# Attention backward on one core: O and wo transposed by DMA, half of K on TensorE

## The chip, the cores and the metric

The kernel runs on one core of a Trainium2 chip. The core has five engines that run at the same time and wait for each other through semaphores: TensorE (PE, matrix multiplies; its weight loads are shown apart as PEld), VectorE (DVE), ScalarE (ACT), GpSimd (POOL) and SyncE (SP), which here issues every DMA. Sixteen DMA engines move data between HBM and the on-chip memory SBUF, and from SBUF to SBUF; a DMA can transpose 128x128 blocks of two-byte data on its way through the crossbar. Matmuls write PSUM, eight banks, from which DVE or ACT copies results to SBUF.

The metric is the device time in microseconds. Of the kernel before there are three runs, median 1665.89 us.

## The reference

Two independent attention blocks A and B, forward and gradients. Only one block's forward is shown; the reference runs it for A and B, concatenates both outputs on the last axis, and takes the gradients of all ten inputs for a given `grad_out`.

```python
B, Sq, D = 8, 96, 640
H, Sk, Dh = 32, 512, 128
q = transpose((x @ wq).reshape(B, Sq, H, Dh), (0, 2, 1, 3))
scores = einsum("bhqd,bhkd->bhqk", q, k_cache) * Dh ** -0.5
p = softmax(scores)
o = einsum("bhqk,bhkd->bhqd", p, v_cache)
out = transpose(o, (0, 2, 1, 3)).reshape(B, Sq, H * Dh) @ wo
...
_out, _vjp = jax.vjp(forward, A_x, A_k_cache, A_v_cache, A_wq, A_wo, B_x, B_k_cache, B_v_cache, B_wq, B_wo)
return (_out, *_vjp(grad_out))
```

All data are bfloat16. The gradients are those of x, of both caches, of wq and of wo.

## The kernel before

One unit of work is a head h and a batch b: 96 queries against 512 keys, 512 units in all (2 blocks x 32 heads x 8 batches). The code does not write instructions in their final order at once. It puts closures into a list, each with a tick and a slot (`Emitter`, L16), sorts by tick and slot and runs them (L25). Unit number n of a block has the tick `ct = tick0 + 8 h + b`, so each head is eight ticks long, and the stages of one unit are spread over the ticks that follow by the table `OFF` (L45): scores at ct+3 (`c_s2a`, `c_s2b`), normalised probabilities at ct+3 (`c_s3b`, on POOL), the transposed probabilities and dV at ct+4 (`c_s45`, `c_s4`), the output O at ct+5, dP and dS at ct+6 (`c_s6`), dK and the transpose of dS at ct+7 (`c_s7`, `c_s8`), dQ at ct+8. In one tick TensorE so works on six units at different stages. A scheduler keeps this order on each engine but for the scores' stages, which have a higher priority, and DMAs marked `pinned` keep the order in which they stand.

Per head there is more work, spread by the table `HK` (L46), whose numbers are ticks relative to the head's first: loads of the head's slices of wq and wo (`pA` at -10, `pA2` at -9), their transposes (`pB` at -3), the projections Q and dO (`pC`), their transposes (`pD`), the transposes of O and dQ to rows of tokens (`qA`, at 18 and 17), and with these the gradients of wo (`qB` at 19 and 20) and of wq (`qD`, for two heads together). Ticks of 8 and more fall into the next heads. For every group of four or five heads there are the matmuls that add the heads' parts to `out` and `dx` (`gU`, L503), spread over some 18 ticks after the group's last unit; stretches of ticks with and without these alternate.

K and V are loaded for two batches at a time: K five ticks ahead of its unit (`OFF["ldk"]`), V three. Both are needed transposed as well. V is always transposed by a DMA from SBUF to SBUF (`c_xt`, tile VT, at the tick of the unit, read six ticks later at L417). For K there are two ways, and `k_on_pe` (L556) chooses: a DMA too (tile KT, three ticks ahead of the unit, read at L298), or TensorE with an identity matrix (`c_s1`, L285, into PSUM, then a DVE copy to the tile KT_pe, L287). Before the change, TensorE has batches 0 and 1 of every head and all batches of the first heads (A0, A1 and B0), which makes 146 of 512; the DMA has 183 pairs of batches.

wo of a head is a tile wo_h of 128x640, that is five blocks. `pB` transposes it on TensorE (L210), and ACT copies the result from PSUM to woT_h (L212, one buffer), which `pC` reads as weights for dO (L243). O of a head is 128x768 in one of the slots of the tile OD, that is six blocks; `qA(h, 0)` transposes it on TensorE (L455), ACT copies it to Onat (L456, one buffer), and `qB` reads it one and two ticks later for dwo (L469).

Order and queues: all DMAs stand in SP's one queue, in the order of their ticks and slots, loads and transposes in slots 0 to 1.7 of a tick. Before it issues a DMA, SP waits for the semaphores of what it needs: the data (an ACT or DVE copy, or an earlier DMA), the buffer's last reader (mostly PE), and the eighth DMA before, since eight semaphores are used in turn. What stands behind a waiting DMA waits with it. PSUM tiles come from one pool of eight banks (`bank`, L98).

Of the kernel before, what the change touches and what calls it, by code (L numbers as in the profile page):

```python
# [11 lines left out]
BF16 = mybir.dt.bfloat16  # L12
# [28 lines left out]
SL_HEAD = 90  # L41
# [1 line left out]
SL_SETUP = 96  # L43

OFF = dict(ldk=-5, ldv=-3, kt=-3, vt=0, s2=3, s3=3, s4=4, s5=5, s6=6, s7=7, s8=8)  # L45
HK = dict(pA=-10, pA2=-9, pB=-3, pC0=[-2, 0], pC1=[-1, 0], pD1=1, pD0=2, qA0=18, qA1=17, qB=[19, 20], qD=[(18, 0, 2), (19, 2, 4), (21, 4, 5)])  # L46
EV = dict(pB0="act", pB1="dve", pC00="act", pC01="act", pC10="act", pC11="dve", pD0="dve", pD1="dve", qA0="act", qA1="dve", qB0="act", qB1="dve", qD="dve", gU="act")
GSPREAD0 = 9
PRIO_OFF = 2000
# [4 lines left out]
def build_block(tc, em, tick0, blk, x, kc, vc, wq, wo, g_all, out_all, dx, dk, dv, dwq, dwo, ident, ones, pools, HG=6, first=True, groups=None):  # L54
    nc = tc.nc
# [42 lines left out]
    def bank(shape, dt, name):  # L98
        return ps.tile(shape, dt, name=name, tag="bank")
# [55 lines left out]
    def evac(eng, dst, src, sc=None):  # L155
        if eng == "act":
            nc.scalar.activation(dst, src, ACT.Identity, scale=(1.0 if sc is None else sc))
        else:
            if sc is None:
                nc.vector.tensor_copy(dst, src)  # L160
            else:
                nc.vector.tensor_scalar(dst, src, float(sc), None, op0=ALU.mult)
# [33 lines left out]
    def pA2(h):  # L196
# [5 lines left out]
            HS[(blk, h)]["wo_h"] = wo_h  # L202
        return f

    def pB(h):
        def f():
            st = HS[(blk, h)]
            woT_ps = bank([128, DC * 128], BF16, "woT_ps")
            for c in range(DC):
                nc.tensor.transpose(woT_ps[:, c * 128:(c + 1) * 128], st["wo_h"][:, c * 128:(c + 1) * 128], ident[:])  # L210
            woT_h = hd.tile([128, DC * 128], BF16, name="woT_h", bufs=1)
            evac(EV["pB0"], woT_h[:], woT_ps[:])  # L212
            st["woT_h"] = woT_h
            wqT_ps = bank([128, DC * 128], BF16, "wqT_ps")
            for c in range(DC):
                nc.tensor.transpose(wqT_ps[:, c * 128:(c + 1) * 128], st["wq_h"][:, c, :], ident[:])
            wqT_h = hst.tile([128, D], BF16, name="wqT_h")
            evac(EV["pB1"], wqT_h[:], wqT_ps[:])
            st["wqT_h"] = wqT_h
            st["slot"] = (blk * H + h) % OD.shape[2]  # L220
            st["OT_h"] = OD[:, 0, st["slot"]]
            st["dQT_h"] = OD[:, 1, st["slot"]]
            st["QT_h"] = hd.tile([128, T], BF16, name="QT_h")
            st["dOT_h"] = hd.tile([128, T], BF16, name="dOT_h")
        return f
# [199 lines left out]
    def c_s7(h, b):  # L425
# [9 lines left out]
            nc.scalar.activation(SB[(blk, h, b // 2, "k")][:, b % 2], dK_ps[:], ACT.Identity, scale=1.0)  # L435
        return f

    def qA(h, which):
        def f():
            st = HS[(blk, h)]  # L440
            src = st["OT_h"] if which == 0 else st["dQT_h"]
            if which == 0:
                dst = hd.tile([128, TT, 128], BF16, name="Onat", bufs=1)
                st["Onat"] = dst
            else:
                if h % 2 == 0:
                    st["dQnat"] = hd.tile([128, TT, 2, 128], BF16, name="dQnat", bufs=1)
                else:
                    st["dQnat"] = HS[(blk, h - 1)]["dQnat"]
                dst = st["dQnat"][:, :, h % 2, :]  # L450
            for t0 in range(0, TT, 8):
                nt = min(8, TT - t0)
                n_ps = bank([128, 8 * 128], BF16, "nat_ps")
                for i in range(nt):
                    nc.tensor.transpose(n_ps[:, i * 128:(i + 1) * 128], src[:, (t0 + i) * 128:(t0 + i + 1) * 128], ident[:])  # L455
                evac(EV["qA%d" % which], dst[:, t0:t0 + nt, :], n_ps[:, 0:nt * 128].rearrange("p (t d) -> p t d", d=128))  # L456
        return f
# [96 lines left out]
    NTS = len(tsplits)  # L554

    def k_on_pe(h, b):  # L556
        return b // NB == 0 or h == 0 or (first and h == 1)

    SX = pools["SX"]
    for g in range(NG):  # L560
        h0 = GH0[g]
        for hh in range(groups[g]):
            h = h0 + hh
            c0t = tick0 + h * B
            if not (first and h == 0):
                em.add(c0t + HK["pA"], SLOTS["LOAD"] + 1.7, pA(h))
                em.add(c0t + HK["pA2"], SLOTS["LOAD"] + 1.7, pA2(h))
            em.add(c0t + HK["pB"], SL_HEAD, pB(h))
            fh = first and h == 0
            p0, p1, d1, d0, late = HK["pC0"], HK["pC1"], HK["pD1"], HK["pD0"], 0  # L570
            if fh:
                p1, d1, d0, late = [3, 3], 3, 4, 7
            elif h == 0:
                p0, p1, d1, d0, late = [-2, 2], [0, 3], 3, 4, 7
            for si in range(NTS):
                em.add(c0t + p0[min(si, 1)], SL_HEAD, pC(h, 0, si))
                em.add(c0t + p1[min(si, 1)], SL_HEAD + late, pC(h, 1, si))
            em.add(c0t + d1, SL_HEAD + (8 if late else 0), pD(h, 1))
            em.add(c0t + d0, SL_HEAD, pD(h, 0))
            for b in range(B):  # L580
                ct = c0t + b
                if b % NB == 0:
                    em.add(tick0 - 12 if first and h == 0 and b == 0 else ct + OFF["ldk"], SLOTS["LOAD"], c_ld(h, b, "K", 7))
                    em.add(ct + OFF["ldv"], SLOTS["LOAD"], c_ld(h, b, "V", 5))
                    if not k_on_pe(h, b):
                        em.add(ct + OFF["kt"], SLOTS["LOAD"] + 1, c_xt(h, b, "KT", 3))
                    em.add(ct + OFF["vt"], SLOTS["LOAD"] + 1, c_xt(h, b, "VT", 4))
                if k_on_pe(h, b):
                    em.add(ct + 2, SLOTS["S1"], c_s1(h, b))
                em.add(ct + OFF["s2"], SLOTS["S2A"], c_s2a(h, b))  # L590
                em.add(ct + OFF["s2"], SLOTS["S2B"], c_s2b(h, b))
                em.add(ct + OFF["s3"], SLOTS["S3A"], c_s3a(h, b))
                em.add(ct + OFF["s3"], SLOTS["S3B"], c_s3b(h, b))
                em.add(ct + OFF["s5"], SLOTS["S5B"], c_s5b(h, b))
                if b % 2 == 1:
                    em.add(ct + OFF["s4"] + 1, SLOTS["LOAD"] + 1.5, c_st(h, b, "v"))
                    em.add(ct + OFF["s7"] + 1, SLOTS["LOAD"] + 1.5, c_st(h, b, "k"))
                em.add(ct + OFF["s4"], SLOTS["S4"], c_s4(h, b))
                for i, o in enumerate(("s8", "s7", "s5", "s4")):
                    SX.setdefault(ct + OFF[o], [None] * 4)[i] = (blk, h, b)  # L600
                em.add(ct + OFF["s6"], SLOTS["S6"], c_s6(h, b))
                em.add(ct + OFF["s7"], SLOTS["S7"], c_s7(h, b))
            hk = HK if first or h < H - 1 else dict(HK, qA0=13, qB=[14, 15], qA1=16, qD=[(19, 0, 2), (19, 2, 4), (19, 4, 5)])
            em.add(c0t + hk["qA0"], SL_HEAD, qA(h, 0))
            for di in range(len(wsplits)):
                em.add(c0t + hk["qB"][di], SL_HEAD + 1, qB(h, di))
            em.add(c0t + hk["qB"][-1] + 1, SLOTS["LOAD"] + 1.6, qB_st(h))
            em.add(c0t + hk["qA1"], SL_HEAD, qA(h, 1))
            for (k_, c_lo, c_hi) in hk["qD"]:
                if c_lo < DC and h % 2 == 1:  # L610
                    em.add(c0t + k_, SL_HEAD + 2, qD(h, c_lo, min(c_hi, DC)))
            if h % 2 == 1:
                em.add(c0t + hk["qD"][-1][0] + 1, SLOTS["LOAD"] + 1.6, qD_st(h))
        cLg = tick0 + (h0 + groups[g] - 1) * B + B - 1
        gs0 = max(3, (GSPREAD0 * groups[g]) // HG)
        gs1 = max(3, (GSPREAD1 * groups[g]) // HG)
        if not first and g == NG - 2:
            gs0, gs1 = 9, 9
        if g == 0:
            em.add(cLg + OFF["s5"] - 2, SL_LOAD, setup_acc)  # L620
        subs = [(0, t, gi) for t in range(TT) for gi in range(len(gsplits))] + [(1, t, gi) for t in range(TT) for gi in range(len(gsplits))]
        n_out = TT * len(gsplits)
        for i, (which, t, gi) in enumerate(subs):
            if which == 0:
                tk = cLg + OFF["s5"] + 2 + (i * gs0) // n_out
            else:
                tk = cLg + OFF["s8"] + 2 + gs0 - 3 + ((i - n_out) * gs1) // n_out
            em.add(tk, SL_GRP, gU(g, which, t, gi))
            if g == NG - 1 and gi == len(gsplits) - 1:
                em.add(tk + 1, SLOTS["LOAD"] + 1.6, gU_st(which, t))  # L630
# [124 lines left out]
```

## Time and profile before

| | |
|---|---|
| median of three runs | 1665.89 us (1665.25 to 1666.51) |
| the profiled execution's own time | 1665.33 us |
| its span, first to last instruction | 1663.6 us |
| instructions | 56195 |
| PE busy | 1645.5 us, 99% |
| ACT busy | 1393.7 us, 84% |
| DVE busy | 1301.9 us, 78% |
| POOL busy | 528.7 us, 32% |
| DMA, mean rate | 264 GB/s, 439.02 MB |
| granted TensorE clock | 1.0 throughout |

The span is the time from the first to the last instruction of one profiled execution; the rest of its time lies around it. A busy engine is one that has an instruction under way. Matmuls are pipelined: the time of one (219 ns for 128 columns in the profile) is longer than the distance to the next, so prices on TensorE are taken from start to start. The chain of waits goes back from the last instruction, at each step to what released it, or to the instruction before it on its engine; the engine with the largest share there sets the time. For a DMA the profile gives the issue on SP and the time from issue to landing. In the timeline a row is: start in us, length in us, engine, source line, operation, output<-inputs, shape, and how many of them were merged.

### The profile page before, as it was taken

Reading aid. Unit: us, or ns where it says so; the run is one execution under the profiler, and the core shown is the slowest. Engines: PE = TensorE matmul, PEld = TensorE weight load, DVE = VectorE, ACT = ScalarE, POOL = GpSimd, SP = SyncE. Lnnn points to the kernel's source line nnn. Section 1 sums busy time; section 2 is a strip of 40 time slices with the busy share of each in tenths; the row PEclk is TensorE's granted clock in tenths of the full one; section 3 lists DMA queues with packets and bytes.
Section 4 is the critical chain, followed back from the end, with each engine's and each line's share of the span. In section 5 each row is a group of like instructions: output and inputs, shape, how many; then the busy total and the mean of one; then the engine's idle time right before and its main releaser. Section 6 shows DMA issues by size and latency. Waiting matters only on the chain.

```text
span 1663.6 us, 56195 instructions
## 1 busy us (share of the span) xinstructions
PE 1645.5 (99%) x21536; PEld 1316.4 (79%) x21536; DVE 1301.9 (78%) x2978; ACT 1393.7 (84%) x3518; POOL 528.7 (32%) x1034
## 2 busy tenths in 40 slices
PE   8999999999999999999999999999999999999999
PEld 6887787787788787877878877877877877877886
DVE  6886677778787788888878867878778778787887
ACT  7999897797798797988868998977977977977975
POOL 2333233333233232333323323323322322332332
PEclk9999999999999999999999999999999999999999
DMA  9999999999999999999999999999999999999994
GB/s 269 257 283 284 255 268 280 249 277 285 217 277 279 245 272 253 276 267 251 292 263 278 294 281 272 278 273 238 276 277 229 287 253 250 258 282 252 281 264 136
DMA packets 811215, 439.02 MB, mean 264 GB/s; under 512 B 483777, under 2 KB 810945, under 8 KB 810945
## 3 DMA queue, kind: packets, MB, share of 16 engines
q1 hardware_dynamic: 810944, 435.43, 107.8%
q8 instruction: 169, 2.77, 0.7%
q14 instruction: 102, 0.83, 0.2%
HBM read 161.09 MB, written 159.12 MB: 192 GB/s over the span
## 4 chain that ended last, share of the span: by engine, by line
PE 78%; ACT 13%; issue 4%; DVE 3%; DMA 1%; POOL 0%; SPq 0%; ACTq 0%; DVEq 0%; POOLq 0%
PE o_ps L514 12%; PE q_ps L243 11%; PE dwq_ps L490 6%; PE dK_ps L432 5%; PE dV_ps L389 5%; PE dP_ps L417 5%; PE S_ps L298 5%; PE dwo_ps L469 5%; PE dst_ps L346 4%; PE x_ps L365 4%; PE x_ps L359 4%; PE x_ps L340 4%; ACT dK_sb L435 3%; ACT E_sb L310 3%; PE n_ps L258 3%
## 5 line engine op out<-in xcount | busy, mean ns | idle before, releaser
L329 POOL TENSOR_SCALAR P_sb<-E_sb,rinv 96x512 bf16<-96x512 bf16 x512 | 354.3, 692 | 1107.8 <-DVE rinv L320 1073.6
L310 ACT ACTIVATE E_sb<-S_ps,negm 96x512 bf16<-96x512 f32 x512 | 354.5, 692 | 160.4 <-DVE negm L300 156.6
L421 DVE SCALAR_TENSOR_TENSOR dS_sb<-dP_ps,dl_ps,P_sb 96x512 bf16<-96x512 f32 x512 | 380.9, 744 | 44.8 <-PE dl_ps L419 40.5
L300 DVE TENSOR_REDUCE negm<-S_ps 96x1 f32<-96x512 f32 x512 | 347.6, 679 | 45.5 <-PE S_ps L298 43.3
L435 ACT ACTIVATE dK_sb<-dK_ps 128x512 bf16<-128x512 f32 x512 | 305.8, 597 | 72.9 <-PE dK_ps L432 71.9
L392 ACT ACTIVATE dV_sb<-dV_ps 128x512 bf16<-128x512 f32 x512 | 314.8, 615 | 0.0
L378 ACT ACTIVATE PT_sb<-x_ps 128x384 bf16<-128x384 bf16 x512 | 256.5, 501 | 0.0
L514 PEld LDWEIGHTS <-OD 128*128 128x128 bf16 x1536 | 135.7, 98 | 103.3 <-issue 1.3
L389 PE MATMUL dV_ps<-dOnat_h,P_sb 96*128 96x128 bf16 x2048 | 198.0, 219 | 1.3 <-DVE dOnat_h L160 0.6
L432 PE MATMUL dK_ps<-Qnat_h,dS_sb 96*128 96x128 bf16 x2048 | 197.8, 219 | 0.0
L417 PE MATMUL dP_ps<-VT,dOT_h 128*96 128x512 bf16 x512 | 195.2, 381 | 0.0
L407 POOL TENSOR_TENSOR prod<-OD,dOT_h 128x96 bf16<-128x96 bf16 x512 | 186.4, 364 | 9.2 <-ACT OD L375 8.2
L348 DVE COPY dST_sb<-dst_ps 128x384 bf16<-128x384 bf16 x512 | 177.2, 346 | 11.9 <-PE dst_ps L346 11.6
L320 DVE RECIPROCAL rinv<-rowsum 96x1 f32<-96x1 f32 x512 | 79.9, 156 | 132.8 <-ACT E_sb L310 128.0
L346 PE MATMUL dst_ps<-ident,dS_sb 96*128 96x96 bf16 x2048 | 171.8, 206 | 2.6 <-DVE dS_sb L421 0.2
L375 ACT ACTIVATE OD<-x_ps 128x192 bf16<-128x192 f32 (+1 forms) x515 | 171.5, 333 | 3.4 <-PE x_ps L340 3.4
L359 PE MATMUL x_ps<-PT_sb,V_sb 128*128 128x96 bf16 x2048 | 172.2, 206 | 0.5 <-ACT PT_sb L378 0.5
L365 PE MATMUL x_ps<-ident,P_sb 96*128 96x96 bf16 x2048 | 171.7, 205 | 0.6 <-POOL P_sb L329 0.3
L340 PE MATMUL x_ps<-dST_sb,K_sb 128*128 128x96 bf16 x2048 | 170.7, 206 | 0.0
L340 PEld LDWEIGHTS <-K_sb 128*128 128x128 bf16 x2048 | 132.6, 98 | 32.1
L514 PE MATMUL o_ps<-wo_h,OD 128*128 128x128 bf16 (+1 forms) x768 | 141.0, 299 | 0.0
L514 PE MATMUL o_ps<-wqT_h,OD 128*128 128x128 bf16 (+1 forms) x768 | 140.0, 299 | 0.2
(75 smaller groups left out, 3224.4 us busy)
## 6 DMA issues: line engine op xcount, KB each, us to landing
out_dram<-dV_sb SPq DMA_DIRECT2D x256, 256.0 KB, 3.6
out_dram<-dK_sb SPq DMA_DIRECT2D x256, 256.0 KB, 3.8
K_sb<-in_A_k_cache_dram SPq DMA_DIRECT2D x128, 256.0 KB, 4.0
V_sb<-in_A_v_cache_dram SPq DMA_DIRECT2D x128, 256.0 KB, 3.9
K_sb<-in_B_k_cache_dram SPq DMA_DIRECT2D x128, 256.0 KB, 4.1
V_sb<-in_B_v_cache_dram SPq DMA_DIRECT2D x128, 256.0 KB, 4.0
out_dram<-dwo_sb SPq DMA_DIRECT2D x64, 160.0 KB, 3.8
out_dram<-dwq_sb SPq DMA_DIRECT2D x32, 320.0 KB, 4.2
```

The lines of the kernel that those rows point to most:

```text
L300: nc.vector.tensor_reduce(negm[:], S_ps[:], axis=AX.X, op=ALU.max, negate=True)
L310: nc.scalar.activation(E_sb[:], st["S_ps"][:], ACT.Exp, bias=st["negm"][:], scale=1.0, accum_out=rowsum[:])
L329: pinned(nc.gpsimd.tensor_scalar(P_sb[:], st["E_sb"][:], st["rinv"][:], 0.0, op0=ALU.mult, op1=ALU.add))
L340: nc.tensor.matmul(dQT_ps, st["K_sb"][:, c, :], st["dST_sb"][:, c * Sq:(c + 1) * Sq], start=(c == 0), stop=(c == KC - 1))
L378: nc.scalar.activation(PT_sb[:], PT_ps, ACT.Identity, scale=1.0)
L389: nc.tensor.matmul(dV_ps[:, c * 128:(c + 1) * 128], P_sb[:, c * 128:(c + 1) * 128], hs["dOnat_h"][:, b * 128:(b + 1) * 128], start=True, s ...
L392: nc.scalar.activation(SB[(blk, h, b // 2, "v")][:, b % 2], dV_ps[:], ACT.Identity, scale=1.0)
L417: nc.tensor.matmul(dP_ps[:], hs["dOT_h"][:, tok], st["VT"], start=True, stop=True)
L421: nc.vector.scalar_tensor_tensor(dS_sb[:], dP_ps[:], dl_ps[:, 0:1], st["P_sb"][:], op0=ALU.subtract, op1=ALU.mult)
L432: nc.tensor.matmul(dK_ps[:, c * 128:(c + 1) * 128], dS_sb[:, c * 128:(c + 1) * 128], hs["Qnat_h"][:, b * 128:(b + 1) * 128], start=True, s ...
L435: nc.scalar.activation(SB[(blk, h, b // 2, "k")][:, b % 2], dK_ps[:], ACT.Identity, scale=1.0)
L514: nc.tensor.matmul(o_ps[:], src[:, t * 128:(t + 1) * 128], rhs, start=(hh == 0), stop=(hh == groups[g] - 1))
```

## The change

Three things are changed. O of every head is transposed by a DMA from its slot in OD to Onat, issued at tick 14 of the head (13 for B's last) in slot 1.2, instead of six TensorE transposes and an ACT copy at tick 18. wo is transposed by a DMA from wo_h to woT_h, issued at tick -6, also in slot 1.2, for all heads but A's first two, which stay on TensorE; woT_h now has two buffers, and its first reader stands at tick -1. And `k_on_pe` now gives TensorE batches 4 and 5 of every head besides batches 0 and 1, so that 122 more units take that way and 61 pairs fewer go through the DMA. For B's last head the two halves of dwo move from ticks 14 and 15 to 16 and 17.

```diff
-HK = dict(pA=-10, pA2=-9, pB=-3, ..., qA0=18, qA1=17, qB=[19, 20], ...)
+HK = dict(pBT=-6, pA=-10, pA2=-9, pB=-3, ..., qT=14, qA1=17, qB=[19, 20], ...)
...
+    def woT_on_pe(h):
+        return first and h < 2
+
+    def pB_xt(h):
+        def f():
+            woT_h = hd.tile([128, DC * 128], BF16, name="woT_h", bufs=2)
+            pinned(nc.sync.dma_start_transpose(woT_h[:].rearrange("p (c k) -> p c k", k=128), HS[(blk, h)]["wo_h"][:]))
+            HS[(blk, h)]["woT_h"] = woT_h
+        return f
+
     def pB(h):
         def f():
             st = HS[(blk, h)]
-            woT_ps = bank([128, DC * 128], BF16, "woT_ps")
-            for c in range(DC):
-                nc.tensor.transpose(woT_ps[:, c * 128:(c + 1) * 128], st["wo_h"][:, c * 128:(c + 1) * 128], ident[:])
-            woT_h = hd.tile([128, DC * 128], BF16, name="woT_h", bufs=1)
-            evac(EV["pB0"], woT_h[:], woT_ps[:])
-            st["woT_h"] = woT_h
+            if woT_on_pe(h):
+                woT_ps = bank([128, DC * 128], BF16, "woT_ps")
+                for c in range(DC):
+                    nc.tensor.transpose(woT_ps[:, c * 128:(c + 1) * 128], st["wo_h"][:, c * 128:(c + 1) * 128], ident[:])
+                woT_h = hd.tile([128, DC * 128], BF16, name="woT_h", bufs=2)
+                evac(EV["pB0"], woT_h[:], woT_ps[:])
+                st["woT_h"] = woT_h
...
+    def qA_xt(h):
+        def f():
+            Onat = hd.tile([128, TT, 128], BF16, name="Onat", bufs=1)
+            pinned(nc.sync.dma_start_transpose(Onat[:], HS[(blk, h)]["OT_h"]))
+            HS[(blk, h)]["Onat"] = Onat
+        return f
+
...
     def k_on_pe(h, b):
-        return b // NB == 0 or h == 0 or (first and h == 1)
+        return b // NB in (0, 2) or h == 0 or (first and h == 1)
...
+            if not woT_on_pe(h):
+                em.add(c0t + HK["pBT"], SLOTS["LOAD"] + 1.2, pB_xt(h))
             em.add(c0t + HK["pB"], SL_HEAD, pB(h))
...
-            hk = HK if first or h < H - 1 else dict(HK, qA0=13, qB=[14, 15], qA1=16, ...)
-            em.add(c0t + hk["qA0"], SL_HEAD, qA(h, 0))
+            hk = HK if first or h < H - 1 else dict(HK, qT=13, qB=[16, 17], qA1=16, ...)
+            em.add(c0t + hk["qT"], SLOTS["LOAD"] + 1.2, qA_xt(h))
```

`qA` keeps only its part for dQ. Instruction counts follow from this: 206 transposes fewer on TensorE, 126 copies fewer on ACT, 122 copies more on DVE, 65 DMAs more in SP's queue.

More of the change, by code (lines that the diff above doesn't have):

```diff
@@ L45 @@
 OFF = dict(ldk=-5, ldv=-3, kt=-3, vt=0, s2=3, s3=3, s4=4, s5=5, s6=6, s7=7, s8=8)
-HK = dict(pA=-10, pA2=-9, pB=-3, pC0=[-2, 0], pC1=[-1, 0], pD1=1, pD0=2, qA0=18, qA1=17, qB=[19, 20], qD=[(18, 0, 2), (19, 2, 4), (21, 4, 5)])
+HK = dict(pBT=-6, pA=-10, pA2=-9, pB=-3, pC0=[-2, 0], pC1=[-1, 0], pD1=1, pD0=2, qT=14, qA1=17, qB=[19, 20], qD=[(18, 0, 2), (19, 2, 4), (21, 4, 5)])
 EV = dict(pB0="act", pB1="dve", pC00="act", pC01="act", pC10="act", pC11="dve", pD0="dve", pD1="dve", qA0="act", qA1="dve", qB0="act", qB1="dve", qD="dve", gU="act")
@@ L440, in f @@
             st = HS[(blk, h)]
[L441 to L444, printed above, removed]
-            else:
[L446 to L450, printed above, removed]
+            src = st["dQT_h"]
+            if h % 2 == 0:
+                st["dQnat"] = hd.tile([128, TT, 2, 128], BF16, name="dQnat", bufs=1)
+            else:
+                st["dQnat"] = HS[(blk, h - 1)]["dQnat"]
+            dst = st["dQnat"][:, :, h % 2, :]
             for t0 in range(0, TT, 8):
@@ L602, in build_block @@
                 em.add(ct + OFF["s7"], SLOTS["S7"], c_s7(h, b))
-            hk = HK if first or h < H - 1 else dict(HK, qA0=13, qB=[14, 15], qA1=16, qD=[(19, 0, 2), (19, 2, 4), (19, 4, 5)])
-            em.add(c0t + hk["qA0"], SL_HEAD, qA(h, 0))
+            hk = HK if first or h < H - 1 else dict(HK, qT=13, qB=[16, 17], qA1=16, qD=[(19, 0, 2), (19, 2, 4), (19, 4, 5)])
+            em.add(c0t + hk["qT"], SLOTS["LOAD"] + 1.2, qA_xt(h))
             for di in range(len(wsplits)):
```

## The prediction

> **What bounds the kernel now.** I read the page's engine line, its DMA line and its chain first.
>
> ```profile
> span 1663.6 us, 56195 instructions
> PE 1645.5 (99%) x21536; PEld 1316.4 (79%) x21536; DVE 1301.9 (78%) x2978; ACT 1393.7 (84%) x3518; POOL 528.7 (32%) x1034
> DMA  9999999999999999999999999999999999999994
> q1 hardware_dynamic: 810944, 435.43, 107.8%
> PE 78%; ACT 13%; issue 4%; DVE 3%; DMA 1%; POOL 0%; SPq 0%; ACTq 0%; DVEq 0%; POOLq 0%
> ```
>
> TensorE is the bound: 78% of the chain. A busy PE is not yet a streaming PE, so I added up what it streams: columns of every matmul over 2.4 columns per ns (128 columns then need 53 ns, and the timeline spaces such transposes by 54 to 57 ns). That gives 1562 us of the 1658 between first and last matmul; 6% is left as per-instruction excess and waits. Two other things stand close. ACT has 13% of the chain, and the DMA queue is full almost everywhere. Chain and timeline show where ACT takes over, in a stretch without group matmuls (the first fence is the chain: start, length, what; the second the timeline of PE):
>
> ```profile
> 1028.38 0.32 ACT OD L375
> 1028.70 0.38 ACT PT_sb L378
> 1029.08 0.48 ACT dV_sb L392
> 1029.56 0.60 ACT Onat L157
> ```
>
> ```profile
> 1030.82 0.16 PE L419 MATMUL dl_ps<-ones,prod 128*96 128x1 bf16 x1
> 1031.03 0.30 PE L469 MATMUL dwo_ps<-g_nat,Onat 128*128 128x320 bf16 x1
> ```
>
> The copy of Onat sits among ACT's regular work, and the first dwo matmul starts 0.21 us after a one-column matmul instead of 0.03. Taken from all starts of PE, waits over 60 ns come to 26.8 us in the steady part, 14.0 us of them in ticks 2 and 3 of each head's eight (a tick here lasts from one S_ps to the next, counted on from the head's first batch), where O is transposed, copied and read.
>
> For the queue, SP's timeline against PE's, at its tightest place:
>
> ```profile
> 927.52 1.24 SPq L275 DMA_TRANSPOSE KT<-K_sb  x1
> ```
>
> ```profile
> 933.07 0.38 PE L298 MATMUL S_ps<-KT,QT_h 128*96 128x512 bf16 x1
> ```
>
> Issue to use is 5.5 us, while a KT takes 4.6 us to land in the median and 6.7 at most. Pairing every KT with its first reader by order, landing to use is 9.7 us in the median, 3.4 at the 5th percentile and 0.3 at the least, here. Slack falls through each stretch without group matmuls (ticks of 2.4 to 2.7 us) and is refilled in the group's stretch (3.2 to 5.0 us): VT's slack runs from 22 down to 7 to 10 us, in block B's first group to 3.4.
>
> **The change, part by part.** TensorE prices are start to start, from the timeline:
>
> ```profile
> 1643.75 0.49 PE L455 MATMUL nat_ps<-ident,OD 128*128 128x128 bf16 x6
> 1644.09 1.52 PE L514 MATMUL o_ps<-wqT_h,OD 128*128 128x512 bf16 x10
> 858.56 0.44 PE L210 MATMUL woT_ps<-ident,wo_h 128*128 128x128 bf16 x5
> 858.83 0.44 PE L216 MATMUL wqT_ps<-ident,wq_p 128*128 128x128 bf16 x5
> ```
>
> and, for K, from the chain:
>
> ```profile
> 1608.23 0.22 PE kT_ps L285 x4
> ```
>
> - O leaves PE: 64 heads x 0.34 us = -21.8 us. ACT loses 64 copies of 820 ns.
> - wo leaves PE for 62 of 64 heads (A's first two stay): 62 x 0.27 = -16.7 us. ACT loses 62 copies of 713 ns; with O's, -96.7 us of ACT.
> - K comes back: batches 4 and 5 of the 61 heads that had them on the crossbar, 122 x 4 transposes: 122 x 0.23 (0.22 in the chain, 4 x 59.7 = 0.24 by mean spacing) = +28.1 us. DVE gains 122 copies of 409 ns, +49.9 us.
> - PE in sum: 206 transposes fewer, -10.4 us. The bounds are small: 206 x 53 ns = 10.9 if all stream, 9.5 with K at 0.24.
>
> Waits. Onat is now issued at tick 14 and read at 19, so dwo has no copy just before it. In front of dwo PE waited 5.7 us in ticks 3, and round the transpose, its PSUM bank and K's about 7 in ticks 2. Least gain 0 (ACT stays late and the wait moves to the next instruction), most 14.0; I take -8: all of the first and a third of the other, since ACT has 0.82 us less in that tick but E_sb, dK and PT_sb keep their order.
>
> DVE. Ticks 6 and 7 get a 0.41 us copy each. In light ticks 6 DVE is busy 2.13 of 2.34 us; it becomes 2.54 of 2.58, and PE already waits 4.7 us there for dS_sb ahead of its transposes. Bounds 0 and +6 (0.1 us per head, 61 heads); I take +2, because the copies fall between S_ps and the next negm and ticks 7 have 0.7 us to spare.
>
> The queue. 61 KT leave; 62 woT of five blocks and 64 Onat of six join: 65 DMAs and 206 blocks more. None of these short transposes is in the trace. The nearest rows:
>
> ```profile
> VT<-V_sb SPq DMA_TRANSPOSE x256, 4.5
> KT<-K_sb SPq DMA_TRANSPOSE x183, 4.6
> ```
>
> Where one was issued over 2 us before its predecessor landed, so that it stood in the queue, it landed 0.95 us (VT) and 0.93 (KT) after it in the median, 1.14 and 1.11 in the mean. From below, by blocks: 61 x -0.93 + 62 x 0.58 + 64 x 0.70 = +24 us. From above, each short one as dear as a full mean one: 65 x 1.11 = +72 us. I take +24: plain DMAs behind others take 0.66 to 0.75 us for 256 KB and 0.48 for 160 KB, so size rules. SP issues them; a transpose occupies it 1.24 us at least and SP's instructions cover 1383 us (83%) of the span, so even 65 x 1.24 = 81 us fits into what is left.
>
> What covers +24 us is the queue's idle time: counting packets from 50 to 1600 us, fewer than eight are in flight during 3.7% = 58 us, fewer than four during 2.5% = 39 us. PE asks 10.4 + 8 us earlier as well, 42 us together: about all of it. Per five-head group (12.8 of them) slack falls by 42/12.8 = 3.3 us at the end of the light stretch. KT then misses in B's first group (0.3 to 2.1 us of slack at four KTs). woT is due sooner than VT of its tick: read one light tick less 0.25 us earlier and landing some 0.8 us later, so its slack is VT's less 3.2: 0.2 at worst now, some -3 after. Once PE has waited, everything behind is early again, so the misses share one price: +4 us. From below 0 (58 us of idle, evenly usable); from above +13 (39 us, and the three groups with KT slack under 3.5 us miss by 4 each). Behind a late VT buffer on SP stand woT, the dV store and the next V and K loads; all keep five ticks of lead. Onat's own waits (OD from tick 12, dwo of the head before, tick 12) are two ticks old when SP comes to tick 14, so they cost nothing; if SP runs 1.4 ticks ahead, as it does with the queue at its emptiest, SP waits there for under a tick, with 20 us of slack behind it.
>
> The last head reads Onat at ticks 16 and 17 instead of 14 and 15, under the same group matmuls; the end still goes dwq, dx, store: 0.
>
> Sum: -10.4 - 8 + 2 + 4 = -12.4 us on the profiled run's 1665.33 (span 1663.6 and 1.7 around it): 1652.9. The median of the runs is 0.56 above that run: 1653.5.
>
> **Rivals.**
> 1. *The queue takes the saving back.* The light stretches become queue-bound: idle 39 us, waits +13, DVE +6, the ACT gain half: -10.4 - 4 + 6 + 13 = +4.6 at worst, about 0 to -5 in the middle: 1663. For it: DMA at 9 in every slice and 0.3 us at the tightest KT. Against: only block B's first group is that tight.
> 2. *Slower: short transposes are priced by the piece.* If five or six blocks cost the queue what eight do (1.11 us), +72 us meet 58 us of idle; from there on the queue, not PE, sets the light stretches, PE's -10.4 - 8 only become waits, and 72 - 58 = +14 us come on top: 1680. It decides as soon as the queue's addition passes 58 us, that is at 1.0 us per short transpose. For it: a fixed part cannot be read from transposes that all have eight blocks. Against: packets pass at one rate, and bytes rule among plain DMAs.
>  The Trainium skill, in "VectorE: DVE Perf Modes", section "Rules for kernel authors", has a 128x128 transpose on TensorE where a PSUM destination will do, and lists 1309 ns for the crossbar; it speaks against this change. By that figure 206 more blocks would be an estimated 270 us of queue, but the trace disagrees: 0.93 us for eight blocks is 0.12 us each in the stream.
> 3. *ACT was the true bound of the light stretches.* Then most of the 26.8 us of waits go with ACT's 96.7: -10.4 - 20 + 2 + 4 = -24: 1641. For it: nothing but ACT stands in the chain after 1028. Against: PE's waits there sum to 14 us.
> That the change misses its aim can be left out: SP issues in program order.
>
> **How the numbers follow.** Forecast 0.52 (its own range 1646 to 1660), rival 1 0.18, rival 2 0.18, rival 3 0.12. A change below 0.2%, 3.3 us, could not be told from none. Faster: 0.52 + 0.12 + 0.07 of rival 1 = 0.71; same: 0.08 of rival 1; slower: 0.18 + 0.03 = 0.21. The range 1642 to 1672 takes in rival 1, nearly all of rival 3 and the lighter third of rival 2.
>
> **What would show it.** nat_ps halves to 384 matmuls, woT_ps falls to 10, kT_ps rises to 1072; ACT falls by about 97 us, DVE rises by 50. Right: dwo starts 0.03 us after dl; gaps of PE, if any, stand before S_ps or q_ps<-gT near 900 to 960 us. Wrong: PE waiting for KT, VT or woT in most groups (rival 1), these waits with short transposes landing over 1.0 us behind their predecessors (rival 2), or no waits in ticks 1 to 6 at all (rival 3).

## The result, and the profile after

The changed kernel takes 1674.13 us in the median of nine runs (1670.27 to 1681.53); the kernel before, in nine runs on the same chip, 1665.61 us (1664.95 to 1666.51). The ratio is 1.0055, with a 95% interval of 1.0045 to 1.0064: slower by 8.5 us. The profiled execution took 1677.57 us, 3.4 more than the median; before it had 1665.33.

These are the lines of its page that answer to those shown of before (line numbers are now those of the changed code: S_ps is L309, dwo L483).

```profile
span 1675.8 us, 55944 instructions
PE 1650.4 (98%) x21330; PEld 1311.1 (78%) x21330; DVE 1346.3 (80%) x3100; ACT 1329.5 (79%) x3392; POOL 529.0 (32%) x1034
DMA  9999999999999999999999999999999999999994
q1 hardware_dynamic: 839392, 442.19, 111.0%
PE 85%; ACT 6%; DVE 3%; DMA 3%; issue 3%; POOL 0%; SPq 0%; ACTq 0%; DVEq 0%; POOLq 0%
```

The page looks better than before: 206 matmuls fewer, ACT 64 us less busy, its share of the chain down from 13 to 6%. What went up is small there: DMA in the chain from 1 to 3%, the queue's packets from 107.8 to 111.0%. The time is lost at few places. In the timeline of PE, the number in brackets is the idle time before the instruction and what ended it:

```profile
820.77 0.16 PE L430 MATMUL dl_ps<-ones,prod 128*96 128x1 bf16 x1
820.80 0.98 PE L483 MATMUL dwo_ps<-g_nat,Onat 128*128 128x320 bf16 x6
824.86 0.71 PE L134 MATMUL tp_ps<-ident,ld_tmp 128*128 128x128 bf16 x5 [3.09 <-DMA ld_tmp<-in_grad_out_dram]
...
936.50 0.66 PE L309 MATMUL S_ps<-KT,QT_h 128*96 128x512 bf16 x1 [2.50 <-DMA KT<-K_sb]
...
1068.25 0.42 PE L309 MATMUL S_ps<-KT,QT_h 128*96 128x512 bf16 x1 [2.06 <-DMA KT<-K_sb]
```

The first two rows show what the change does reach: dwo starts 0.03 us after dl (0.02 at the place shown of before, where it was 0.21). The other three are the waits, all of them for a transfer: grad_out's tile for block B's first transposes, and KT twice. Each has a tail. These are the stretches of low clock at the three waits; the first two begin before the wait is over, the third 1.2 us after it (start:end, length, busy time of each engine, then the granted clock, DMA share and GB/s):

```profile
823.70:830.50 6.80, 5.06 (x42) 4.40 (x43) 2.94 (x7) 1.08 (x3) 0.51 (x1) 0.50 1.00 301
...
936.30:939.70 3.40, 3.20 (x23) 2.33 (x24) 1.60 (x4) 0.88 (x3) 0.01 (x1) 0.50 1.14 356
...
1069.40:1072.80 3.40, 3.40 (x33) 2.89 (x31) 1.72 (x4) 2.57 (x6) 1.05 (x2) 0.50 1.13 359
```

The clock is 0.50 for 3.4 us (6.8 after the longest wait), where the page's row of forty slices shows 9 throughout. Laid side by side by the starts of dP, the changed kernel is 2.0 us behind at its first head, 0.7 at head 31, and then jumps to +6.4, +9.7 and +12.9 us at these three places; it ends 12.8 us behind.

How did these transfers come to be late? SP's timeline before the second wait:

```profile
926.11 1.30 SPq L286 DMA_TRANSPOSE VT<-V_sb  x1
927.51 1.26 SPq L452 DMA_TRANSPOSE Onat<-OD  x1
928.86 0.53 SPq L409 DMA_DIRECT2D out_dram<-dV_sb  x1
929.48 0.48 SPq L512 DMA_DIRECT2D out_dram<-dwq_sb  x1
930.06 0.55 SPq L277 DMA_DIRECT2D V_sb<-in_B_v_cache_dram  x1
930.70 0.48 SPq L277 DMA_DIRECT2D K_sb<-in_B_k_cache_dram  x1
931.24 2.16 SPq L286 DMA_TRANSPOSE KT<-K_sb  x1
```

Each row starts some 0.1 us after the end of the one before: SP doesn't wait, it issues without a pause and is behind. And an issue doesn't get cheaper with the tile. In the view of one tile (duration in ns, minimum/median/maximum):

```profile
L211 SPq DMA_TRANSPOSE woT_h<-wo_h x62: 1206/1388/2879, 34.6 to 1603.3; - x62
...
L452 SPq DMA_TRANSPOSE Onat<-OD x64: 1215/1502/3197, 45.0 to 1655.7; - x64
...
L286 SPq DMA_TRANSPOSE KT<-K_sb x122: 1237/1253/2538, 49.2 to 1627.0; - x122
```

Five blocks hold SP for 1.21 us at least, six for 1.22, eight (the two K of a KT) for 1.24. In the mean a transpose holds it longer, 1.5 us before (663 us for 439) and after (773 us for 504); no run shows why, and the full engines may hold an issue back. SP's instructions cover 1501 us now, 1383 before; its pauses of over 0.1 us, the real waits, fall from 161 to 48 us in all. The 16 DMA engines are as full: fewer than eight packets are in flight for 12 us between 50 and 1600 us, before for 58.

### The profile page after: what moved, and what is told of

Same layout as the page of the kernel before. It is cut to its first block, busy times and chain, and to the rows that moved or that the text cites. A ratio compares the mean times of both kernels' runs of the same rounds, so it can differ in the third digit from the quotient of the medians.

```text
span 1675.8 us, 55944 instructions
## 1 busy us (share of the span) xinstructions
PE 1650.4 (98%) x21330; PEld 1311.1 (78%) x21330; DVE 1346.3 (80%) x3100; ACT 1329.5 (79%) x3392; POOL 529.0 (32%) x1034
## 3 DMA queue, kind: packets, MB, share of 16 engines
q1 hardware_dynamic: 839392, 442.19, 111.0%
## 4 chain that ended last, share of the span: by engine, by line
PE 85%; ACT 6%; DVE 3%; DMA 3%; issue 3%; POOL 0%; SPq 0%; ACTq 0%; DVEq 0%; POOLq 0%
PE q_ps L254 13%; PE o_ps L528 12%; PE dK_ps L443 6%; PE dwq_ps L504 6%; PE S_ps L309 6%; PE dV_ps L400 6%; PE dP_ps L428 6%; PE dwo_ps L483 5%; PE dst_ps L357 5%; PE x_ps L370 5%; PE x_ps L376 4%; PE x_ps L351 4%; PE n_ps L269 3%; PE kT_ps L296 3%; ACT E_sb L321 2%
## 5 line engine op out<-in xcount | busy, mean ns | idle before, releaser
L321 ACT ACTIVATE E_sb<-S_ps,negm 96x512 bf16<-96x512 f32 x512 | 348.9, 682 | 227.6 <-DVE negm L311 219.3
L446 ACT ACTIVATE dK_sb<-dK_ps 128x512 bf16<-128x512 f32 x512 | 300.1, 586 | 71.7 <-PE dK_ps L443 67.6
L403 ACT ACTIVATE dV_sb<-dV_ps 128x512 bf16<-128x512 f32 x512 | 308.8, 603 | 0.0
L389 ACT ACTIVATE PT_sb<-x_ps 128x384 bf16<-128x384 bf16 x512 | 250.5, 489 | 0.0
L359 DVE COPY dST_sb<-dst_ps 128x384 bf16<-128x384 bf16 x512 | 176.6, 345 | 10.2 <-PE dst_ps L357 10.0
L386 ACT ACTIVATE OD<-x_ps 128x192 bf16<-128x192 f32 (+1 forms) x515 | 165.4, 321 | 3.8 <-PE x_ps L351 3.8
```

Source lines behind the costliest of these rows:

```text
L321: nc.scalar.activation(E_sb[:], st["S_ps"][:], ACT.Exp, bias=st["negm"][:], scale=1.0, accum_out=rowsum[:])
L403: nc.scalar.activation(SB[(blk, h, b // 2, "v")][:, b % 2], dV_ps[:], ACT.Identity, scale=1.0)
```

## The experiments

Medians, beside the kernel before on the same chip (1665.2 to 1665.8 us); ratios with their 95% intervals.

### The parts alone

K alone, to the kernel before (`e1_k_only`):

```diff
-        return b // NB == 0 or h == 0 or (first and h == 1)
+        return b // NB in (0, 2) or h == 0 or (first and h == 1)
```

> Only K's part of the change: batches 4 and 5 of 61 heads on TensorE, O and wo stay on TensorE. Theory (light ticks and queue: in ticks without group matmuls DVE and ACT set the pace, so PE's transposes cost or save there only in part, and the rest of the loss comes from a full queue): 122 ticks longer by 0.25 us as in the changed kernel's ticks 6 and 7, +30 us, the queue with 57 us less to do and no wait for a DMA: 1695 us. Rival (the queue held the kernel before back, and relief of it pays): under 1685 us.

1690.91 us, ratio 1.0150 (1.0135 to 1.0165), between what the theory and the rival said. PE has no wait of over 0.15 us for KT, and fewer than eight packets are in flight for 9.2% of the time. So K's half costs 25 us and leaves the queue roomy.

O and wo by DMA, K back at a quarter (`e2_o_wo_k_quarter`, from the changed kernel):

```diff
-        return b // NB in (0, 2) or h == 0 or (first and h == 1)
+        return b // NB == 0 or h == 0 or (first and h == 1)
```

> O and wo by DMA, K stays at a quarter on TensorE. The queue gets 45 + 36 = 81 us more against 58 us of idle before. Theory: the queue is full throughout, PE waits for KT, VT or woT in most groups, savings on PE (38 us) cannot be taken: 1675 to 1695 us. Rival (only the three waits of the changed kernel matter, PE's savings are real everywhere): 1665.6 - 38 + 15 = about 1643 us.

1747.60 us, ratio 1.0490 (1.0474 to 1.0506). Its waits of PE (what waits, total us, times, longest):

```profile
PE S_ps L309 <- DMA KT<-K_sb: 53.5, 37, 3.6
PE dwo_ps L483 <- DMA Onat<-OD: 9.2, 9, 2.2
PE q_ps L254 <- DMA woT_h<-wo_h: 8.5, 8, 1.6
```

With 126 more transposes and nothing taken away the queue sets the time: 82 us more, in waits all along the kernel, and 53 us over the theory's highest figure. The K that the change moves to PE pays for the room that O and wo take.

O alone, and wo alone, both with K at a quarter. `e3_o_only` is the changed kernel with

```diff
     def woT_on_pe(h):
-        return first and h < 2
+        return True
```

and K as in the diff above; `e4_wo_only` keeps `woT_on_pe` and leaves O's transposes in `qA`.

> O alone by DMA, K at a quarter, wo on TensorE. Theory: the saving of 0.33 us is taken only in the some 42 heads whose tick 2 also has group or dwq matmuls, -14 us; the queue gets 45 us more and costs one or two waits of 3 to 5 us: 1652 to 1662 us. Rival (saving everywhere): 1665.6 - 21.8 = 1644 us and less.

> wo alone by DMA (62 heads), K at a quarter, O on TensorE. Theory: -7 us in the 18 heads whose tick 5 has group matmuls, -5 us in the others; the queue gets 36 us more, one or two waits: 1655 to 1662 us. Rival (saving everywhere): 1665.6 - 16.7 = 1649 us and less.

O alone: 1665.15 us, 1.0003 (0.9987 to 1.0019), single runs from 1662 to 1675. wo alone: 1672.19 us, 1.0046 (1.0030 to 1.0063). Both miss the theory's range, which ended at 1662 us. In both profiled executions most of the waiting sits where the changed kernel has it: for KT or grad_out near 818, 919, 931 and 1084 us (O) and near 810, 820, 932 and 940 us (wo); further waits stand near 130 us (O) and at 270 and 727 us (wo). Between them O alone gains 0.32 us in each tick 2 that has other matmuls beside it, 41 times, and 0.02 us in each light tick 2.

### What in the queue is full

Four kinds of plain DMA issued from GpSimd instead of SP: the loads of wq and wo, the stores of dwo and dwq (`e5_plain_on_pool`, from the changed kernel; `e8_ow_quarter_pool` is the same edit on `e2_o_wo_k_quarter`). One of the four lines:

```diff
-            pinned(nc.sync.dma_start(dwo[h * 128:(h + 1) * 128, :], HS[(blk, h)]["dwo_sb"][:]))
+            pinned(nc.gpsimd.dma_start(dwo[h * 128:(h + 1) * 128, :], HS[(blk, h)]["dwo_sb"][:]))
```

> The changed kernel, with the loads of wq and wo and the stores of dwo and dwq issued from GpSimd's queue, not SP's: the same bytes on the same 16 DMA engines, 191 issues fewer on SP. Theory S (SP's issuing is what is full: a transpose holds SP for 1.21 us at least, with five blocks as with eight, and SP's waits for others fell from 161 to 48 us): SP gets some 110 us back, PE's long waits for KT and ld_tmp vanish, 1660 to 1666 us, if GpSimd's own issuing does not delay P_sb. Theory B (the 16 engines and their bytes are full): the long waits stay, 1670 to 1678 us.

> O and wo by DMA, K at a quarter on TensorE, and the loads of wq and wo and the stores of dwo and dwq from GpSimd's queue. Against the same kernel with all on SP (1747.6 us). Theory S: SP's issuing falls by 110 us to about the changed kernel's, PE has 28 us less than there: 1650 to 1680 us. Theory B: the bytes are the same and the queue stays full: over 1725 us.

1691.59 us (1.0149, 1.0126 to 1.0172) and 1750.66 us (1.0523, 1.0475 to 1.0570). Nothing is won, and the first lies above both theories. SP issues 190 DMAs fewer, but its instructions don't cover less time: 1528 us, 1501 in the changed kernel, since the transposes that stay hold it for 880 us, not 773 (1602 and 1586 us in the other pair). The 16 engines stay full (fewer than eight packets 0.5% and 0.6% of the time), and in the first of them the transposes land further apart: VT 1.38 us behind its predecessor in the mean, 1.24 in the changed kernel. POOL also pays 0.59 to 0.92 us for each issue, beside P_sb. So the edit didn't take the load off SP that it was to take off, and it doesn't decide between SP and the engines.

wo's transpose in two pieces, the same bytes (`e6_wot_in_two`):

```diff
-            pinned(nc.sync.dma_start_transpose(woT_h[:].rearrange("p (c k) -> p c k", k=128), HS[(blk, h)]["wo_h"][:]))
+            woT_v, wo_v = woT_h[:].rearrange("p (c k) -> p c k", k=128), HS[(blk, h)]["wo_h"][:]
+            pinned(nc.sync.dma_start_transpose(woT_v[:, 0:3], wo_v[:, 0:384]))
+            pinned(nc.sync.dma_start_transpose(woT_v[:, 3:5], wo_v[:, 384:640]))
```

> The changed kernel with each wo transpose split into two DMAs of three and two blocks: the same bytes, 62 pieces more. Theory S (by the piece on SP): 62 x 1.3 = 80 us more on SP, which has 48 us left: 1690 to 1720 us, with waits for KT in most groups. Theory B (by the byte): within 5 us of the changed kernel, 1670 to 1680 us.

1739.08 us, 1.0450 (1.0423 to 1.0478). The chain and the two halves in the view of the tile:

```profile
PE 78%; DMA 11%; ACT 5%; DVE 3%; issue 2%; SPq 1%; POOL 0%; ACTq 0%; DVEq 0%; POOLq 0%
```

```profile
L212 SPq DMA_TRANSPOSE woT_h<-wo_h x62: 1207/1265/2404, 32.8 to 1664.4; - x62
L213 SPq DMA_TRANSPOSE woT_h<-wo_h x62: 1236/1240/2337, 34.0 to 1665.8; - x62
```

Three blocks and two blocks hold SP as long as eight. 62 more pieces cost 65 us against the changed kernel, 1.05 us each, more than either theory said. SP's instructions cover 1569 us, 68 more, and its real waits are down to 35 us, while the engines have more idle time again (3.8%). With no byte more, this price is by the piece, and here SP's issuing sets it. The Trainium skill, "Perfetto Trace Analysis", section "What "DMA-bound" means", names the issuing engine's sequencer and the DMA engines as two separate bounds; the runs agree, and the changed kernel is close to both.

### VectorE or ScalarE in the light ticks

Two copies moved from DVE to ACT (`e7_copies_to_act`, from the changed kernel):

```diff
-EV = dict(pB0="act", pB1="dve", ..., pD0="dve", ...)
+EV = dict(pB0="act", pB1="act", ..., pD0="act", ...)
```

> The changed kernel with the PSUM copies of Qnat, dOnat's partner at tick 2 (678 ns), and of wqT at tick 5 (479 ns) on ACT, not DVE: 64 of each. Theory D (in light ticks DVE sets the pace, so O's and wo's savings on PE were lost there): light ticks 2, 3 and 5 get shorter, 17 x 0.3 and 42 x 0.15 = -11 us, of which the fuller queue takes some back: 1662 to 1670 us. Rival A (ACT sets the pace there): longer, over 1676 us.

1678.45 us, 1.0081 (1.0065 to 1.0098), runs 1674 to 1680: in all no better, and by its time on the side of rival A. It still has waits for the queue, of 4.0 us for KT at 936 us, so the ticks tell more than the time. The windows of the same two light ticks, 2 and 3 of head 38 (columns: length, PE, PEld, DVE, ACT, POOL, clock), first before:

```profile
1025.96:1028.64 2.68, 2.68 (x49) 2.49 (x47) 2.68 (x7) 2.57 (x9) 1.18 (x3) 1.00 1.17 327
1028.64:1031.17 2.53, 2.48 (x43) 2.21 (x42) 2.53 (x7) 2.53 (x7) 0.75 (x2) 1.00 1.23 147
```

the changed kernel:

```profile
1035.14:1037.82 2.68, 2.67 (x46) 2.33 (x44) 2.68 (x7) 2.57 (x9) 1.18 (x3) 1.00 1.16 342
1037.82:1040.45 2.63, 2.63 (x39) 2.21 (x40) 2.63 (x6) 2.00 (x6) 0.74 (x2) 1.00 1.44 72
```

and with the copies on ACT:

```profile
1034.53:1037.27 2.74, 2.65 (x44) 2.27 (x41) 2.72 (x7) 2.74 (x9) 1.30 (x3) 1.00 1.19 252
1037.27:1039.71 2.44, 2.38 (x36) 2.01 (x37) 2.15 (x6) 2.44 (x6) 0.75 (x2) 1.00 1.15 232
```

In tick 2 DVE is busy for the whole length, 2.68 of 2.68 us, before and after: O's transposes are gone from PE and the tick is as long as it was. What ends it can be read where the next S_ps starts. Its K is transposed on TensorE, so it needs DVE's copy KT_pe, first before, then in the changed kernel:

```profile
1028.18 0.40 DVE L287 COPY KT_pe<-kT_ps 128x512 bf16<-128x512 bf16 x1
...
1028.64 0.38 PE L298 MATMUL S_ps<-KT_pe,QT_h 128*96 128x512 bf16 x1
```

```profile
1037.36 0.40 DVE L298 COPY KT_pe<-kT_ps 128x512 bf16<-128x512 bf16 x1
...
1037.82 0.42 PE L309 MATMUL S_ps<-KT_pe,QT_h 128*96 128x512 bf16 x1
```

S_ps starts 0.05 to 0.07 us after the end of that copy in all 17 light ticks 2, in both kernels. DVE, which is busy nearly without a pause up to there, so ends the tick, whether PE has O's six transposes in it or not.

In tick 3 the change takes O's copy from ACT (2.53 to 2.00) and DVE then fills the tick, 2.63 of 2.63. Taking a copy from DVE (Qnat's falls here, not in tick 2 as expected) shortens tick 3 by 0.22 us in the mean of 17 such ticks (2.64 to 2.41), and ACT fills it. That DVE sets light tick 3 of the changed kernel is so shown. The copies of wqT fall in ticks 6 and 0 of these stretches: 26 light ticks 6 get 0.08 us shorter, 10 light ticks 0 0.16 us longer.

### Place and amount

Around the start of block B, O of 12 heads and wo of 12 heads back on TensorE (`e9_spare_b`, from the changed kernel, both numbered through both blocks; of the edit, the two functions that choose the heads):

```diff
+    def o_on_dma(h):
+        return (h if first else H + h) in set(range(64)) - set(range(29, 41))
     def woT_on_pe(h):
-        return first and h < 2
+        return (h if first else H + h) in {0, 1} | set(range(31, 43))
```

> The changed kernel, but around the start of block B (O of heads 29 to 40 of the 64, wo of heads 31 to 42) both are transposed on TensorE again; K stays at a half. Theory W (three waits in B's first third and the half clock after each make the loss): TensorE's waits for grad_out's transposes near 820 us and for KT near 936 and 1068 us shrink to those of the kernel before (under 1 us each); -13 us for these, and +6 us for the heads put back (8 heavy ticks x 0.33 + 12 x 0.27): about 1667 us. Rival F (the queue as a whole is full, and a wait removed here comes back at the next place where its slack is out): waits of the same kind turn up after 1100 us, 1673 us or more.

1670.55 us, 1.0026 (1.0016 to 1.0037), single runs 1667 to 1675. In the profiled execution (1668.15 us, one of the shorter ones) the three waits are gone, as theory W said, and one of 1.3 us at 255 us is left; that execution is 9.4 us shorter than the changed kernel's. Yet it isn't below the kernel before. So the waits are only a part of the loss, and W's sum, 1667 us, was short by 3.5.

K at a quarter, wo on TensorE, O by DMA in 35 heads: those whose transposes fall in a tick of over 3.0 us, none near B's start (`e10_o_group`, here against `e3_o_only`). `e11_ow_group` adds wo of 15 heads chosen in the same way.

```diff
     def o_on_dma(h):
-        return True
+        return (h if first else H + h) in set([1, 3, 4, 5, 7, 9, 10, 11, 13, 14, 15, 17, 19, 20, 21, 23, 24, 25, 27, 28, 41, 42, 43, 45, 46, 47, 49, 51, 52, 53, 55, 56, 57, 59, 61])
```

> The kernel before with one thing changed: O is transposed by DMA in 35 of the 64 heads, those whose transposes fall in a tick longer than 3.0 us in the kernel before, without the heads around the start of block B; wo on TensorE, K at a quarter. Theory P (O's transposes are worth 0.33 us in ticks with other TensorE work and nothing in light ticks, where VectorE is busy all the time; the queue takes 35 more DMAs if they stay away from B's start): -0.33 x 35 = -11.6 us, +2 us for waits: about 1656 us, no wait of TensorE for KT over 1 us after 100 us. Rival F (the queue has no room at any place): waits for KT appear in other groups, 1663 us or more.

> As the run before it, and wo by DMA in 15 heads whose transposes of wo fall in a tick longer than 3.0 us, again none around B's start. Theory P: the queue's idle time in the kernel before is 58 us and 50 short transposes take about 45 of it, so 15 x 0.38 = -5.7 us more than the run before: about 1650 us. Rival F, or a threshold: what the queue still has free is not to be had evenly, KT waits come back and the time is 1656 us or more.

`e10_o_group`: 1654.76 us, 0.9933 (0.9921 to 0.9945), runs 1653.8 to 1655.5. It beats the kernel before by 11 us and the changed kernel by 19. Its page and its waits:

```profile
span 1653.1 us, 55625 instructions
PE 1624.7 (98%) x21147; PEld 1305.0 (79%) x21326; DVE 1300.3 (79%) x2978; ACT 1368.6 (83%) x3483; POOL 527.2 (32%) x1034
```

```profile
PE S_ps L312 <- DMA KT<-K_sb: 1.1, 2, 0.8
```

The ticks 2 with group or dwq matmuls are 10.9 us shorter in sum, light ticks unchanged; -11.6 was expected. `e11_ow_group`: 1662.84 us, 0.9984 (0.9970 to 0.9999), runs from 1656 to 1670. Theory P's 1650 fell: 15 more short transposes, and in its profiled execution waits of over 0.9 us (from start to start) are back at 617, 713, 784 to 814, 1432 and 1583 us. The queue's idle time can't be used up to its last microsecond. Where it is nearly used up the time varies from one execution to the next: over 14 us here, under 2 with 15 DMAs fewer.

### The change with a queue that has room

Every second store of dV left out, in the changed kernel (`e12_after_half_dv`) and in the kernel before (`e13_before_half_dv`):

```diff
-                        em.add(ct + OFF["s4"] + 1, SLOTS["LOAD"] + 1.5, c_st(h, b, "v"))
+                    if b % 4 == 1:
+                        em.add(ct + OFF["s4"] + 1, SLOTS["LOAD"] + 1.5, c_st(h, b, "v"))
```

> The changed kernel without every second store of dV (128 of 256 left out, so half of dV is not written); nothing else differs. That frees the queue of about 128 x 0.5 to 0.7 = 64 to 90 us, more than the 57 us that the change added to it, and no work of TensorE, VectorE or ScalarE changes. Theory Q+D (two losses: the queue's waits with the half clock behind them, about 13 us, and VectorE, which sets the light ticks and lets the rest of the gain go by): the waits vanish and the time falls to 1658 to 1663 us. Rival Q alone (the queue took all, and TensorE's saving of 10.4 us and 8 us of waits was there otherwise): 1653 us or less, light tick 2 shorter by 0.3 us. Rival C (the loss is TensorE's clock or the chip, not the queue): unchanged near 1674 us.

> The kernel before without the same 128 stores of dV (half of dV is not written): the other side of the comparison. It waits little for the queue (KT 3.9 us in all, start-up aside), so 1661 to 1665 us by every theory; the difference between this run and the run before it is what the change would be worth with a queue that has room: Q+D says -1 to -5 us, Q alone -10 to -18 us, C +8 us.

1663.58 us (0.9986, 0.9978 to 0.9995) and 1665.43 us (0.9999, 0.9990 to 1.0008). The kernel before gains nothing from an emptier queue; the changed kernel gains 10.5 us, DMA is down from 3 to 1% of the chain, and after the first 20 us PE waits for no transfer over 0.5 us:

```profile
span 1659.9 us, 55412 instructions
...
PE 86%; ACT 6%; DVE 4%; issue 3%; DMA 1%; POOL 0%; SPq 0%; ACTq 0%; DVEq 0%; POOLq 0%
```

So the loss splits: 10.5 us for the queue (1674.1 - 1663.6), and without it the change is worth -1.9 us (1663.6 - 1665.4), as theory Q+D said. The intervals of the two ratios touch, so the gain is small at most; the -10 us and more of rival Q are out. That difference, tick by tick from the traces of the two, whose executions differ by 3.5 us (units 24 to 500 of 512; a tick is numbered as in the code, modulo 8, so that S_ps of batch b opens tick b + 3; light means under 3.0 us before; expected is the change in transposes times 0.055 us):

| tick of the head | times | expected, us in all | measured, us in all |
|---|---|---|---|
| 2, with group or dwq matmuls (O leaves) | 42 | -13.9 | -14.9 |
| 2 and 3, light (O leaves; its copy goes) | 17 + 17 | -5.6 | +1.9 |
| 5 with group matmuls, light 4 and 5 (wo leaves) | 18 + 39 + 42 | -16.5 | -17.3 |
| 6 and 7 with group matmuls (K joins) | 34 + 33 | +14.3 | +16.6 |
| 6 and 7, light (K joins) | 26 + 26 | +11.4 | +13.3 |
| light 1 and the rest | | 0 | -2.4 |
| sum | | -10.2 | -2.8 |

## Why the prediction was wrong, step by step

The forecast was -12.4 us; the medians differ by +8.5. Two steps failed. The gain on TensorE and in its waits was credited also in ticks that DVE ends (with DVE's own term -16.4 us forecast, -1.9 measured). And the queue's addition was priced at 24 us where it took about 58 (+4 forecast, +10.5 measured).

- *TensorE, -10.4.* Counts and prices were right: 206 transposes fewer, and by the table 0.35 us per head for O where PE sets the tick (14.9 in 42), 0.29 for wo and 0.26 per unit for K. The step that failed is to credit them everywhere. In the light ticks 2 and 3 DVE has no time left (2.68 of 2.68 us), so 5.6 us of O's saving didn't come and the ticks got 1.9 us longer; why longer isn't shown. The forecast asked this of DVE for ticks 6 and 7, where K's copies go, and not for the ticks where the saving was to be.
- *Waits, -8.* The first half of its reading was right, dwo now follows dl at once; but the wait moved on, as the lower bound of 0 had it. At the place shown, dl now starts 0.37 us after dP, before 0.22, and in tick 2 PE waits for DVE's KT_pe where O's transposes stood. What was seen as ACT's lateness in the copy of Onat was a tick in which DVE and ACT were both full (2.53 of 2.53 us each). Of the 8 us, light tick 1 gave 2.4 and the heavy ticks 2 another 1.
- *DVE, +2.* K's copies cost 4.2 us over the matmuls' price in ticks 6 and 7 (13.3 + 16.6 - 11.4 - 14.3), inside the bounds of 0 to 6. Taken together, the three steps promised -16.4 and gave -1.9.
- *The queue, +4.* It cost 10.5. The addition was priced at 24 us by blocks; the queue's idle time fell from 58 to 12 us while the span grew by 12, so its work grew by about 58. The pair without half of dV says the same (127 to 65 us, with a span 3.5 us shorter). The short transposes themselves landed as far behind their predecessors as their size said (woT 0.55 us, Onat 0.66 in the median; 0.58 and 0.70 forecast; 62 x 0.67 + 64 x 0.80 - 61 x 1.11 = +25 by the means). What was missing seems to be that all others came further apart: VT 1.145 to 1.239 us in the mean, KT 1.107 to 1.212, 378 of them, an estimated 37 us. That is argued, not shown: in the pair without half of dV, VT's distance grows (1.17 to 1.24) and KT's doesn't (1.15 to 1.10). SP's room was overrated too. Of its 280 us of pauses, 119 are the 45 ns between any two instructions, so 161 were to be had, and its transposes took 110 us more, not 81: the forecast used the least time of an issue for all.
- *ACT and DVE in sum.* ACT lost 64.2 us, not 96.7, and DVE gained 44.4, not 49.9: the forecast multiplied lengths, and instructions of an engine overlap in the profile (Onat's copy is 0.82 us long and stands in the chain with 0.60).
- *The clock.* No term had it. At each of the three waits TensorE ran at half clock for 3.4 us or more, which is part of the 10.5 us.
- *The places.* One of three was right, KT at 936 us in B's first group; the waits at 824 us (grad_out) and 1068 us (KT) were not named. The last head's move cost nothing to be seen.

Of the rivals, the second had the queue's price: it decides at 58 us of addition, and the addition came to 58. Its 1680 us is nearer than the forecast, but its sign, short transposes landing over 1.0 us behind their predecessors, did not come (0.67 and 0.80 us), and its picture, a queue that sets every light stretch, is that of the split transposes and of O and wo with K at a quarter; in the changed kernel's profiled execution the queue shows in three late transfers alone. The rule that it quotes from the Trainium skill ("VectorE: DVE Perf Modes", section "Rules for kernel authors"), TensorE where a PSUM destination will do, holds here only in part: 35 of O's transposes are better on the DMA, by 11 us. The third rival falls: with 64 us less of ACT, the light ticks stayed. The first was right that the saving would be taken back, but the queue took only half of what was lost: 10.5 of the 20.9 us between forecast and result, 4 of them forecast.

Open is how the queue's 10.5 us divide between SP's issuing and the 16 engines: both were nearly full, the run meant to take load off SP left its instructions covering as much time, and leaving out half of dV frees both.

## What to carry to other kernels

Ask of each tick or stage that an edit shortens which engine is full there; an average of 78% hid a DVE that was busy for all of 2.68 us, so the same six transposes were worth 0.33 us in one tick and nothing in the next. Move to the DMA only what pays and only where the queue has slack: 35 transposes gained 11 us, 64 gained nothing, 126 less 61 lost 8.5. Price a DMA transpose by the piece on its issuing engine as well as by its bytes, and count an idle queue as room only as far as the transfers with the least slack allow.

## What the runs showed of the hardware that was not expected

A transpose holds SP for 1.21 to 1.24 us at least whether it has two, three, five, six or eight blocks. TensorE's granted clock fell to 0.5 for 3.4 us behind 2.06 us of idleness (at 1068 us in the changed kernel) and behind 2.01 us (931 us, O alone), while 2.48 us left it at 1.0 in another place (818 us, O alone): the length of the wait doesn't decide by itself. Over the traces of all runs, none of PE's idle times under 1.77 us (after the first 20 us) was followed by it, all 17 above 3.04 us were, and those between went either way. The Trainium skill, "TensorE: Matmul & The Clock Gate", section "Part 1: The HAM clock gate (the "warmup" mystery)", has a free-running window of about 3.4 us, and the fall after one idle window. The 3.4 us of the low clock agree, and a free-running window would fit that the length alone doesn't decide, but a wait much shorter than the window, 1.77 us at 392 us with the plain DMAs on GpSimd, was enough here. And leaving out 128 stores of 256 KB from the kernel before, whose DMA row shows 9 in every slice, changed its time by nothing (0.9999): a row of nines is no proof of a bound.
